# Turning round the product of keys and inputs in a two-branch linear attention kernel, with the gate as a weight column, queries interleaved, and first loads reordered

## The chip, the cores and the metric

The kernel runs on one core of a Trainium2 chip. The metric is the device time of one execution in microseconds (us), as a median of several. A profile of one execution has its own length, called the span; here the time is 1.3 us over the span. Every execution is marked fast or slow (slow: more than 1.5% above the fastest of the same kernel), and fast ones are compared with fast ones.

## The reference

Two linear attention blocks, A and B, read the same x of 2048 x 640. They have their own weights and 32 heads of 20. A gate mixes their outputs.

```python
def block(x, wqkv, wo):                  # A and B alike
    q, k, v = split_heads(x @ wqkv)      # 32 heads of 20
    phi = lambda t: where(t > 0, t + 1, exp(t)) + 1e-6
    pq, pk = phi(q), phi(k)
    kv  = einsum("bhsd,bhse->bhde", pk, v)
    z   = einsum("bhsd->bhd", pk)
    num = einsum("bhqd,bhde->bhqe", pq, kv)
    den = einsum("bhqd,bhd->bhq", pq, z) + 1e-6
    return merge_heads(num / den) @ wo
g = sigmoid((x * gate_w).sum(-1))
return g * block_A(x) + (1 - g) * block_B(x)
```

## The kernel before

The values are never formed. With G = x^T pk, the product of keys and values is pk^T v = G^T Wv, masked to the heads' blocks. This is multiplied by Wo into a matrix WP per block. An output tile is then scaled pq times WP, summed over A and B; the scale holds gate and denominator.

TensorE goes through these stages: 32 key units (5 pairs of a 512- and a 128-column matmul each), 10 G units (16 pairs each) with the small products between them, 40 query units (5 matmuls of 512 columns each), two denominators, 16 output tiles (10 pairs each). ScalarE takes exponentials and copies from PSUM. VectorE finishes phi, sums keys over the sequence, multiplies x by the gate weights, and scales the queries. A small scheduler in Python fixes the order of instructions on each engine when the kernel is built. The queues in the profile are q1 (SP, hardware), q10 (ACT, hardware) and q0 (POOL, software).

The first loads, with cuts:

```python
dma("SP", "x0", XN[:, 0, :], x[0:128, :], ...)
dma("POOL", "cst", CST[:, :], cap[:, :], ...)              # identity and masks
for c in range(NC):
    dma("ACT", "wkA%d" % c, WK["A"][:, c, :], wqkv["A"][...], ...)
dma("SP", "x1", XN[:, 1, :], x[128:256, :], ...)
dma("POOL", "wkB", WK["B"], w3("B", 1), 819200, ...)        # one load of 800 KB
xt_dma(256, 512)                                            # DMA transposes, on SP
xt_dma(512, 1024); xt_dma(1024, 1536); xt_dma(1536, 2048)
dma("SP", "gwb", ...); dma("SP", "xr", XN[:, 2:NT, :], ...) # then WV, WQ, WO
```

G, and the mask of the product of keys and values, with cuts:

```python
def g_unit(X, c):                        # G: rows are inputs, columns keys
    for t in range(NT):
        l = XN[:, t, 128 * c : 128 * c + 128]
        e.matmul(a[:, 0:512], l, PKt[X][:, t, 0:512], ...)
        e.matmul(a[:, 512:D], l, PKt[X][:, t, 512:D], ...)

def kv_unit(X):                          # after the matmuls
    e.tensor_tensor(out=KVL[X][:, us[0] : us[0] + n, :],
        in0=PS[0:GR, ps.slot, 0 : GR * n].rearrange("p (u f) -> p u f", u=n),
        in1=BDM.unsqueeze(1).to_broadcast([GR, n, GR]), op=ALU.mult)
```

The order of TensorE: all G units, then all queries. They must follow, since the finished queries PQ lie in the memory of the keys PK.

Of the kernel before, what the change touches and what calls it, by code (L numbers as in the profile page):

```python
# [7 lines left out]
ALU = mybir.AluOpType  # L8
# [20 lines left out]
def _consts():  # L29
    p = np.arange(128)[:, None]  # L30
    ident = (p == np.arange(128)[None, :]).astype(np.float32)
    bd = (p // 20 == np.arange(GR)[None, :] // 20).astype(np.float32)
    zm = (p // 4 == np.arange(H)[None, :]).astype(np.float32)
    return _bf16_bits(np.concatenate([ident, bd, zm], axis=1))


CW = 128 + GR + H
# [34 lines left out]
class Sched:  # L72
# [12 lines left out]
    def run(self):  # L85
# [26 lines left out]
        while len(self.order) < n:  # L112
# [25 lines left out]
            if o.dma:  # L138
                at[e] = w + o.dma[0]
                o.end = max(w + o.dma[0] + 1500.0, bus[0]) + o.dma[1] / 330.0  # L140
                bus[0] = max(w + o.dma[0] + 1500.0, bus[0]) + o.dma[1] / 330.0
            else:
                o.end = at[e] = w + o.cost
                if e == "PE":
                    o.end += 160.0
# [98 lines left out]
def body(nc, A_x, A_wqkv, A_wo, B_x, B_wqkv, B_wo, gate_w, out, log=None):  # L244
# [9 lines left out]
    XN = sb("XN", [128, NT, D], bf)  # L254
    WKW = sb("WKW", [128, 2 * NU * D], bf)
    WK = {X: WKW[:, i * NC * D : (i + 1) * NC * D].rearrange("p (c f) -> p c f", c=NC) for i, X in enumerate(XS)}
# [5 lines left out]
    PQ = {X: PK[X][:, :].rearrange("p (g s) -> p g s", g=NC) for X in XS}  # L262
# [4 lines left out]
    FX = {(X, b): sb("FX%s%d" % (X, b), [128, 512], bf) for X in XS for b in range(NB)}  # L267
# [4 lines left out]
    ZA = {X: sb("ZA" + X, [128, D], f32) for X in XS}  # L272
    ZH = sb("ZH", [128, 2, D], bf)
# [6 lines left out]
    GWB = sb("GWB", [128, D], bf)  # L280
    GSC = sb("GSC", [128, D], bf)
    LG = sb("LG", [128, NT], f32)
# [12 lines left out]
    BDM = CST[0:GR, 128 : 128 + GR]  # L295
    ZMK = CST[:, 128 + GR : CW]

# [6 lines left out]
    def dma(q, name, dst, src, nbytes, ins=(), outs=(), after=(), issue=450.0, transpose=False):  # L304
        def fn(e):
            d = dst() if callable(dst) else dst
            with nc.allow_non_contiguous_dma(reason="layout"):
                return e.dma_start(d, src() if callable(src) else src, transpose=transpose)

        return op(q, fn, 0.0, ins, outs, after, name=name, dma=(issue, nbytes))  # L310
# [24 lines left out]
    dma("SP", "x0", XN[:, 0, :], x[0:128, :], 163840, outs=[bxn[0]])  # L335
    dma("POOL", "cst", CST[:, :], cap[:, :], 71680, outs=[bcst], issue=700.0)
    for c in range(NC):
        dma("ACT", "wkA%d" % c, WK["A"][:, c, :], wqkv["A"][128 * c : 128 * c + 128, D : 2 * D], 163840, outs=[bwk["A", c]])
    dma("SP", "x1", XN[:, 1, :], x[128:256, :], 163840, outs=[bxn[1]])

    def xt_dma(r0, r1):
        dma(
            "SP",
            "xt%d" % r0,
            XT[:, :, r0:r1],
            x[r0:r1, :],
            (r1 - r0) * D * 2,
            outs=bxt[r0 // 128 : r1 // 128],
            issue=(r1 - r0) * 12.0,
            transpose=True,  # L350
        )
# [4 lines left out]
    dma("POOL", "wkB", WK["B"], w3("B", 1), 819200, outs=[bwk["B", c] for c in range(NC)], issue=900.0)  # L356
    xt_dma(256, 512)
    xt_dma(512, 1024)
    xt_dma(1024, 1536)
    xt_dma(1536, 2048)  # L360
    dma("SP", "gwb", GWB[:, :], gate_w.rearrange("(o n) -> o n", o=1).partition_broadcast(128) if False else gate_w.partition_broadcast(128), 163840, outs=[bgwb])
    dma("SP", "xr", XN[:, 2:NT, :], x[256:S, :].rearrange("(t p) d -> p t d", p=128), 14 * 163840, outs=bxn[2:])
    for X in XS:
        dma("SP", "wv" + X, WV[X][:, :, :], w3(X, 2), 819200, outs=[bwv[X]])
    for X in XS:
        dma("SP", "wq" + X, WQ[X][:, :, :], w3(X, 0), 819200, outs=[bwq[X]])
# [8 lines left out]
    for i in range(7):  # L375
        op(
            "PE",
            lambda e: e.matmul(psw(bw, 512), ONE[:, 0:128], ONE[:, :], start=True, stop=True),
            430.0,
            ins=[bone],  # L380
            outs=[bw],
            name="warm",
        )
    for t in range(2):
        for piece in ((0, 2), (2, 5)):
            bt = Buf("tp", "ps")
            lo, hi = piece
# [16 lines left out]
            def cp(e, t=t, lo=lo, hi=hi, tv=tv):  # L404
                i = tv()[:, 0 : 128 * (hi - lo)].rearrange("p (c s) -> p c s", c=hi - lo)
                o = XT[:, lo:hi, 128 * t : 128 * t + 128]
                if lo == 0:
                    return e.tensor_copy(o, i)
                return e.activation(o, i, ACT.Copy)

            half = Buf("xth")
            op("DVE" if lo == 0 else "ACT", cp, 350.0 if lo == 0 else 510.0, ins=[bt], outs=[half], name="tpc%d" % t)
            bxt[t].halves = getattr(bxt[t], "halves", []) + [half]

# [3 lines left out]
    def k_unit_steps(X, t, ps):  # L418
        def step(c):
            def fn(e):  # L420
                a = psw(ps, D)
                l = XT[:, c, 128 * t : 128 * t + 128]
                e.matmul(a[:, 0:512], l, WK[X][:, c, 0:512], start=(c == 0), stop=(c == NC - 1))  # L423
                return e.matmul(a[:, 512:D], l, WK[X][:, c, 512:D], start=(c == 0), stop=(c == NC - 1))  # L424

            xin = [bxt[t]] if not hasattr(bxt[t], "halves") else [bxt[t].halves[0 if c < 2 else 1]]
            op("PE", fn, mm_cost(512) + mm_cost(128), ins=xin + [bwk[X, c]], outs=[ps], name="k%s%d_%d" % (X, t, c))

        return step

    def k_post(X, t, ps):
# [4 lines left out]
        op("ACT", lambda e: e.activation(EK[:, ek.slot, :], psw(ps, D), ACT.Exp), act_cost(D), ins=[ps], outs=[ek], name="ke")  # L436
# [17 lines left out]
    for X in XS:  # L454
        pss = [Buf("k", "ps", 2) for _ in range(2)]
        st = [k_unit_steps(X, t, pss[t]) for t in range(2)]
        if X == "A":
            for c in range(NC):
                for t in range(2):
                    st[t](c)  # L460
        else:
            for t in range(2):
                for c in range(NC):
                    st[t](c)
        for t in range(2):
            k_post(X, t, pss[t])
    for t in range(2, NT):
        for X in XS:
            ps = Buf("k", "ps", 2)
            s = k_unit_steps(X, t, ps)  # L470
            for c in range(NC):
                s(c)
            k_post(X, t, ps)
# [3 lines left out]
    bsc = None  # L477
    blg = []
    for t in range(NT):
        b = Buf("lg%d" % t)  # L480
        blg.append(b)
        nsc = Buf("gsc")
        op(
            "DVE",
            lambda e, t=t: e.scalar_tensor_tensor(
                GSC[:, :], XN[:, t, :], 1.0, GWB[:, :], op0=ALU.mult, op1=ALU.mult, accum_out=LG[:, t : t + 1]
            ),
            dve1(D) + 100,
            ins=[bxn[t], bgwb] + ([bsc] if bsc else []),
            outs=[b, nsc],  # L490
            prio=LOW + t,
            name="lg",
        )
        bsc = nsc
    bge, bge2, bgg, bgg2, bgt = Buf("ge"), Buf("ge2"), Buf("gg"), Buf("gg2"), Buf("gt")
    op("ACT", lambda e: e.activation(GE[:, :], LG[:, :], ACT.Exp, scale=-1.0), 250.0, ins=blg, outs=[bge], prio=LOW, name="ge")
    op("DVE", lambda e: e.tensor_scalar(GG[:, 1, :], GE[:, :], 1.0, None, op0=ALU.add), 150.0, ins=[bge], outs=[bge2], prio=LOW + 50, name="ge1")
# [5 lines left out]
        ins=[bgg, bge, bge2],  # L503
# [29 lines left out]
    bza = {}  # L533
    for X in XS:
        prev = None
        for t in range(1, NT):
            n = Buf("za%s%d" % (X, t))
            if t == 1:
                f = lambda e, X=X: e.tensor_tensor(out=ZA[X][:, :], in0=PKt[X][:, 0, :], in1=PKt[X][:, 1, :], op=ALU.add)
                ins = [bpk[X, 0], bpk[X, 1]]  # L540
            elif t < NT - 1:
                f = lambda e, X=X, t=t: e.tensor_tensor(out=ZA[X][:, :], in0=ZA[X][:, :], in1=PKt[X][:, t, :], op=ALU.add)
                ins = [prev, bpk[X, t]]
            else:
                f = lambda e, X=X, t=t: e.tensor_tensor(
                    out=ZH[:, XS.index(X), :], in0=ZA[X][:, :], in1=PKt[X][:, t, :], op=ALU.add
                )
                ins = [prev, bpk[X, t]]
            op("DVE", f, dve1(D), ins=ins, outs=[n], prio=LOW + 100 + 20 * XS.index(X) + t, name="za")
            prev = n  # L550
        bza[X] = prev


    bgs = {}

    def g_unit(X, c):
        ps = Buf("g", "ps", 2)
        for t in range(NT):

            def fn(e, t=t):  # L560
                a = psw(ps, D)
                l = XN[:, t, 128 * c : 128 * c + 128]
                e.matmul(a[:, 0:512], l, PKt[X][:, t, 0:512], start=(t == 0), stop=(t == NT - 1))  # L563
# [368 lines left out]
```

## Time and profile before

| | before |
|---|---|
| time, median (3 runs) | 212.49 us |
| span of the profile | 211.6 us |
| first G matmul (end of the key stage) | 64.5 us |
| TensorE waits for key weights | 12.6 us |
| TensorE waits on VectorE, 150 to 168 us | 4.7 us |

The page of the kernel before: the busy line, then rows of 40 equal slices of 5.3 us. A digit is the busy share in tenths; PEclk is the clock granted to TensorE, GB/s what the DMA engines moved.

```profile
PE 190.0 (90%) x1311; PEld 105.9 (50%) x1311; DVE 134.1 (63%) x231; ACT 75.2 (36%) x116; POOL 1.8 (1%) x7
...
PE   5402999999999999999999999999966899999995
...
PEclk9955699999999999999999999999999999999999
DMA  6999999999500002102214045000300015111111
GB/s 182 87 84 123 222 163 318 362 347 239 133 0 3 0 2 60 45 0 61 58 46 151 0 116 179 18 0 26 99 0 0 34 40 176 66 62 62 65 62 64
```

Counted from 1, TensorE is dense but for slices 1 to 4 and a dip at slices 30 to 32. In the first gap the DMA engines are 90% busy, yet move only 84 to 123 GB/s in slices 3 and 4, against some 350 later.

The start in stages (windows). Columns: stretch and length, busy time of TensorE (instructions), granted clock, DMA share (a sum over overlapping packets, so it can pass 1), GB/s.

```profile
core 0: us, PE busy (x), PEclk, DMA share, GB/s
...
9.00:20.00 11.00, 0.14 (x2) 0.59 1.24 108
20.00:24.75 4.75, 4.28 (x15) 0.50 0.98 180
```

From 9 to 20 us TensorE does next to nothing (0.14 us). Then it works at half the clock until 24.75 us.

The same stretch from the SP queue (timeline: start, duration, what was issued):

```profile
0.74 0.89 SPq L308 DMA_DIRECT2D XN<-in_A_x_dram  x2
1.69 26.48 SPq L308 DMA_TRANSPOSE XT<-in_A_x_dram  x4
```

Four transposes take 26.5 us to issue. Looked at singly, the second takes 16.35 us of that, and the last two 3.3 us each.

The queues at 9 to 20 us (packets, MB, time of their packets as a share of the 16 engines):

```profile
q1 hardware_dynamic: 1040, 0.26, 86.3%
q0 software_dynamic: 143, 0.68, 20.9%
q10 hardware_dynamic: 224, 0.25, 16.9%
```

The 1,040 packets of q1, nearly all of the transposes, take 86% of 16 engines for 11 us. That is 0.15 us for a packet of 250 bytes, as a mean. The packed trace, read packet by packet, shows that they are not all slow: half of them took 18 ns, and the 323 that took more than 0.2 us hold 83% of the time.

TensorE's idle places (timeline; in brackets the idle time before the line and what ended it):

```profile
8.43 0.38 PE L423 MATMUL ps<-WKW,XT 128*128 128x512 bf16 x1 [1.23 <-DMA WKW<-in_A_wqkv_dram]
20.03 0.61 PE L423 MATMUL ps<-WKW,XT 128*128 128x512 bf16 x1 [10.89 <-DMA WKW<-in_A_wqkv_dram]
...
156.25 5.59 PE L650 MATMUL ps<-XT,WQB 128*128 128x512 bf16 x25 [2.07 <-DVE PKB L676]
163.74 1.52 PE L820 MATMUL ps<-WPA,PKA 128*128 128x512 bf16 x10 [1.90 <-DVE PKB L676]
167.34 0.39 PE L721 MATMUL ps<-PKA,ZBD 128*32 128x512 bf16 x1 [0.73 <-DVE PKB L676]
```

### The profile page before, as it was taken

How to read it: one execution, taken by the hardware profiler on the slowest of the kernel's cores; microseconds unless marked ns; L12 is line 12 of the kernel's file. 1: busy time of each engine (PE TensorE's matmuls, PEld its weight loads, DVE VectorE, ACT ScalarE, POOL GpSimd, SP SyncE). 2: the span in 40 equal slices, each digit the busy share in tenths (PEclk: the TensorE clock that was granted, in tenths of full speed). 3: DMA queues.
4: the chain of work that ended last, by engine and by line, in shares of the span. 5: the costliest groups of instructions: out<-in, count | busy, mean ns of one | idle time of the engine just before them, and what ended most of it. 6: DMA issues, size and time to landing. Idle time of an engine off the chain costs nothing.

```text
span 211.6 us, 3143 instructions
## 1 busy us (share of the span) xinstructions
PE 190.0 (90%) x1311; PEld 105.9 (50%) x1311; DVE 134.1 (63%) x231; ACT 75.2 (36%) x116; POOL 1.8 (1%) x7
## 2 busy tenths in 40 slices
PE   5402999999999999999999999999966899999995
PEld 1200455555555555575556655545523455555553
DVE  0100488999999999989605878999999674600000
ACT  2100355555552211113333695555236322222222
POOL 3000000000000000000000000000000000000000
PEclk9955699999999999999999999999999999999999
DMA  6999999999500002102214045000300015111111
GB/s 182 87 84 123 222 163 318 362 347 239 133 0 3 0 2 60 45 0 61 58 46 151 0 116 179 18 0 26 99 0 0 34 40 176 66 62 62 65 62 64
DMA packets 22596, 19.86 MB, mean 94 GB/s; under 512 B 10470, under 2 KB 21894, under 8 KB 22582
## 3 DMA queue, kind: packets, MB, share of 16 engines
q1 hardware_dynamic: 21654, 17.95, 35.0%
q10 hardware_dynamic: 720, 0.82, 2.1%
q0 software_dynamic: 208, 0.89, 1.7%
q8 instruction: 10, 0.16, 0.3%
q14 instruction: 4, 0.03, 0.0%
HBM read 12.83 MB, written 4.54 MB: 82 GB/s over the span
## 4 chain that ended last, share of the span: by engine, by line
PE 76%; DVE 12%; DMA 9%; ACTq 1%; issue 0%; ACT 0%; DVEq 0%
PE ps L820 19%; PE ps L563 16%; PE ps L423 16%; PE ps L650 11%; DMA WKW<-in_A_wqkv_dram 9%; PE ps L564 4%; PE ps L424 4%; DVE PKB L676 3%; DVE PKA L676 3%; DVE EQ L668 2%; DVE RCT L751 2%; PE ps L581 2%; DVE PKB L777 1%; DVE PKA L777 1%; PE ps L616 1%; PE ps L721 1%
## 5 line engine op out<-in xcount | busy, mean ns | idle before, releaser
L423 PE MATMUL ps<-WKW,XT 128*128 128x512 bf16 x160 | 45.8, 391 | 12.6 <-DMA WKW<-in_A_wqkv_dram 12.6
L424 PE MATMUL ps<-WKW,XT 128*128 128x128 bf16 x160 | 35.7, 223 | 0.0
L436 ACT ACTIVATE EK<-ps 128x640 bf16<-128x640 f32 x32 | 22.4, 703 | 36.4 <-PE ps L424 36.4
L423 PEld LDWEIGHTS ps<-WKW,XT 128*128 128x128 bf16 x160 | 16.0, 100 | 33.4 <-DMA WKW<-in_A_wqkv_dram 12.2
L665 ACT ACTIVATE EQ<-ps 128x512 bf16<-128x512 f32 x40 | 23.9, 598 | 23.5 <-PE ps L650 13.8
L820 PE MATMUL ps<-WPA,PKA 128*128 128x512 bf16 (+1 forms) x160 | 24.5, 299 | 1.9 <-DVE PKB L676 1.9
L650 PE MATMUL ps<-XT,WQB 128*128 128x512 bf16 x100 | 22.9, 379 | 2.1 <-DVE PKB L676 2.1
L820 PE MATMUL ps<-WPB,PKB 128*128 128x512 bf16 (+1 forms) x160 | 24.5, 299 | 0.0
L439 DVE TENSOR_SCALAR EK<-EK 128x640 bf16<-128x640 bf16 x32 | 10.4, 325 | 20.2 <-ACT EK L436 20.2
L650 PE MATMUL ps<-XT,WQA 128*128 128x512 bf16 x100 | 22.8, 379 | 0.0
L842 ACT ACTIVATE OST<-ps 128x640 bf16<-128x640 f32 (+1 forms) x16 | 11.1, 696 | 32.2 <-PE ps L820 32.2
L563 PE MATMUL ps<-PKB,XN 128*128 128x512 bf16 x80 | 22.3, 379 | 0.0
L563 PE MATMUL ps<-PKA,XN 128*128 128x512 bf16 x80 | 21.8, 379 | 0.0
L668 DVE TENSOR_SCALAR EQ<-EQ 128x512 bf16<-128x512 bf16 x40 | 11.5, 288 | 13.1 <-ACT EQ L665 12.3
L820 PEld LDWEIGHTS ps<-WPA,PKA 128*128 128x128 bf16 x160 | 12.3, 98 | 12.1 <-issue 2.8
L564 PE MATMUL ps<-PKA,XN 128*128 128x128 bf16 x80 | 17.5, 219 | 0.0
L564 PE MATMUL ps<-PKB,XN 128*128 128x128 bf16 x80 | 17.5, 219 | 0.0
L650 PEld LDWEIGHTS ps<-XT,WQB 128*128 128x128 bf16 x100 | 11.4, 118 | 11.7 <-DVE PKB L676 2.5
L820 PEld LDWEIGHTS ps<-WPB,PKB 128*128 128x128 bf16 x160 | 12.3, 98 | 9.4
L840 DVE CAST OST<-ps 128x128 bf16<-128x128 f32 x1 | 0.3, 291 | 26.3 <-PE ps L820 26.3
L650 PEld LDWEIGHTS ps<-XT,WQA 128*128 128x128 bf16 x100 | 11.4, 118 | 9.5 <-issue 0.4
L424 PEld LDWEIGHTS ps<-WKW,XT 128*128 128x128 bf16 x160 | 16.0, 100 | 0.0
(65 smaller groups left out, 199.6 us busy)
## 6 DMA issues: line engine op xcount, KB each, us to landing
out_dram<-OST SPq DMA_DIRECT2D x15, 160.0 KB, 1.8
XN<-in_A_x_dram SPq DMA_DIRECT2D x1, 2240.0 KB, 11.6
WKW<-in_A_wqkv_dram ACTq DMA_DIRECT2D x5, 160.0 KB, 6.6
WKW<-in_B_wqkv_dram POOLq DMA_DIRECT2D x1, 800.0 KB, 19.7
WVA<-in_A_wqkv_dram SPq DMA_DIRECT2D x1, 800.0 KB, 13.4
WVB<-in_B_wqkv_dram SPq DMA_DIRECT2D x1, 800.0 KB, 13.6
WQA<-in_A_wqkv_dram SPq DMA_DIRECT2D x1, 800.0 KB, 11.7
WQB<-in_B_wqkv_dram SPq DMA_DIRECT2D x1, 800.0 KB, 13.0
```

The lines of the kernel that those rows point to most:

```text
L423: e.matmul(a[:, 0:512], l, WK[X][:, c, 0:512], start=(c == 0), stop=(c == NC - 1))
L424: return e.matmul(a[:, 512:D], l, WK[X][:, c, 512:D], start=(c == 0), stop=(c == NC - 1))
L436: op("ACT", lambda e: e.activation(EK[:, ek.slot, :], psw(ps, D), ACT.Exp), act_cost(D), ins=[ps], outs=[ek], name="ke")
L439: lambda e: e.tensor_scalar(EK[:, ek.slot, :], EK[:, ek.slot, :], 1.0, EPS, op0=ALU.min, op1=ALU.add),
L563: e.matmul(a[:, 0:512], l, PKt[X][:, t, 0:512], start=(t == 0), stop=(t == NT - 1))
L564: return e.matmul(a[:, 512:D], l, PKt[X][:, t, 512:D], start=(t == 0), stop=(t == NT - 1))
L650: r = e.matmul(PS[:, ps.slot, :], WQ[X][:, c, g::5], XT[:, c, 512 * b : 512 * b + 512], start=(c == 0), stop=(c == NC - 1),)
L665: op("ACT", lambda e: e.activation(EQ[:, eq.slot, :], PS[:, ps.slot, :], ACT.Exp), act_cost(512), ins=[ps], outs=[eq], name="qe")
L668: lambda e: e.tensor_scalar(EQ[:, eq.slot, :], EQ[:, eq.slot, :], 1.0, EPS, op0=ALU.min, op1=ALU.add),
L676: lambda e: e.scalar_tensor_tensor(PQ[X][:, g, 512 * b : 512 * b + 512], PS[:, ps.slot, :], 0.0, EQ[:, eq.slot, :], op0=ALU.max, op1=ALU.add),
L820: r = e.matmul(a[:, l0 - lo : h0 - lo], PQ[X][:, g, 128 * t : 128 * t + 128], WP[X][:, g, l0:h0], start=(i == 0 and g == 0), stop=(i == 1 ...
L842: op("ACT", lambda e, w=w, ps=ps, os_=os_: e.activation(OST[:, os_.slot, 0:w], psw(ps, w), ACT.Copy), act_cost(w), ins=[ps], outs=[os_], n ...
```

## The change

Its intent: shorten the start; take the sums of keys and the gate products (39 us) off VectorE; move queries forward among the G units, so that VectorE isn't flooded later.

- The key weights go in single chunks over the SP and ACT queues, ahead of all transposes. A third tile of x is transposed by TensorE.
- G^T is computed. Strided slices of pk are stationary and x moves, with a column of ones that gives z. The result is copied out and turned back by ten DMA transposes from SBUF to SBUF.
- gate_w is a 641st column of B's key weights; the gate's exponential reads it from PSUM.
- Queries have memory of their own at first, so 25 of 40 units go among the G units. The scalings are put at fixed places in VectorE's order.
- The rows of the product are now ordered by g and m (key 5m+g). The mask multiplication puts them back.

The main edits, with cuts:

```diff
+    dma("ACT", "cst", CST[:, :], cap[:, :], 128 * CW * 2, outs=[bcst])
+    ld_x("SP", 1)
+    ld_wk("ACT", "A", 0)
+    ld_wk("SP", "A", 1)
+    ld_wk("ACT", "A", 2)
+    ld_x("SP", 2)
+    ld_wk("ACT", "A", 4)
+    ld_wk("SP", "A", 3)
+    dma("ACT", "gw", GW5[:, :], ...)
+    for c in range(NC):
+        ld_wk("SP", "B", c)
+    for t0, t1 in ((3, 4), (4, 5), (5, 6), (6, 8), (8, 12), (12, 16)):
+        xt_dma(t0, t1)
 ... (in g_unit)
-                l = XN[:, t, 128 * c : 128 * c + 128]
-                e.matmul(a[:, 0:512], l, PKt[X][:, t, 0:512], ...)
+                l = PKt[X][:, t, g::5]
+                e.matmul(a[:, 0:512], l, XN[:, t, 0:512], ...)
+                return e.matmul(a[:, 512 : D + 1], l, XN[:, t, 512 : D + 1], ...)
+        dma("SP", ..., GS[X][:, :, 128 * g : 128 * g + 128], GTS[X][:, g, :], transpose=True)
 ... (in kv_unit)
-                    out=KVL[X][:, us[0] : us[0] + n, :],
+                    out=KVL[X][:, us[0] : us[0] + n, :].rearrange("p u (m g) -> p u g m", g=NC),
 ... (order; the sums of keys, the gate products and z_unit are gone)
+    for g in range(NC):
+        g_unit("A", g); q_next(3)
+    for g in range(NC):
+        g_unit("B", g); q_next(2)
+        ...                                  # A's products at g = 1 to 4
+    q_next(1); den(0); q_next(3)
+    kv_unit("B"); q_next(3)
+    for u in range(NU):
+        wp_unit("B", u)
+        if u % 2: q_next(1)
+    wp_back("B"); q_next(1); scale_now(0); q_next(4)
+    out_unit(0); scale_now(1); den(1)
```

## The prediction

> **What bounds it now.** TensorE: busy 190.0 of 211.6 us (busy table). The span cut into stages (windows) shows three losses.
> 1. Start. The key projection issues only 6 of its 160 matmul pairs by 9 us, waits for the A key weights until 20.0 us (waits: 12.6 us, longest 10.9), and runs at a granted clock of 0.50 until 24.75. The culprit is not volume: the DMA view moves 353 GB/s at 3 to 5 us, but 108 GB/s at 9 to 20 us with the engines busy. The second DMA transpose, issued beside weight loads still in flight on two other queues, holds its queue for 16.35 us; the last two take 3.3 us each. The Trainium skill ("DMA: Bandwidth & Descriptors", Issuing engines are not separate DMA queues) says that all queues share the same 16 engines; this agrees.
> 2. 150 to 168.5 us: VectorE is over 95% busy (reciprocal 3.35 us, scaling 1.49 us each, query post-processing 0.98 us per unit against 1.08 us of TensorE); TensorE loses 4.7 us.
> 3. The tail after the last matmul, 2.0 us.
>
> Elsewhere TensorE is dense: a 512+128 pair is 0.271 us, 160 pairs 43.4 us; a query unit is 1.08 us.
>
> **What the change does.**
> - First loads: weights go ahead of all transposes on two hardware queues. 2.2 MB at 353 GB/s from 2.2 us: A weights by about 7 us, B by 9 us; then the transposes run alone, 13 tiles at about 1 us each (a 4-tile one now issues in 3.3 us and lands in 5.9). The first transposed tile is needed near 13.5 us, then one per 2.7 us, so they keep ahead. The key stage should start at 5.2 us, lose 1 to 2 us in arrivals, and end near 50 us, against 64.5 now: minus 14.5 us, all on the critical path and nearly all of the gain.
> - G^T has the same 160 pairs (129 columns for 128). Stationary slices now step by 5. The Trainium skill ("TensorE: Matmul & The Clock Gate", Weight-path perf modes) allows fast weight load at such steps. In the trace, ten strided loads feeding one-column matmuls pass in 0.36 us, so I expect the pair to stay at 0.27 us.
> - The sums of keys (30 x 0.82 us) and the gate products (16 x 0.9 us) leave VectorE: 39 us, none on the path. ScalarE gains 16 small exponentials (about 0.2 us each). Worth nearly nothing; dropping the z matmuls saves 0.36 us.
> - Ten SBUF transposes of 164 KB, about 4 us each to landing, with 8 us or more of other TensorE work ahead of their use: hidden.
> - 25 query units move among G, out of the VectorE-bound stage. But after the first denominator VectorE still owes 14 units, the reciprocal, masks and two scalings: 22.6 us, against 18.4 us of TensorE. Before the first output tile they are about equal. I expect 3 us (0 to 6) of stall to remain of the 4.7.
>
> **Sum.** Key stage ends 50; then 139.9 us of dense work (145.1 now, less 4.9 stall, 0.36 z); 3 stall; 2 tail: span 195. The time is about 1 us over the span: 196 us. Range 191.5 to 201.5. Chances: faster 0.96, same 0.03, slower 0.01.
>
> **Right if** the wait for key weights falls below 2 us, the first G matmul starts at 49 to 52 us, its pair stays at 0.27 us, VectorE busy falls to about 97 us, and stalls around the first output tile total 0 to 6 us.
>
> **Wrong if** transposes again starve other loads, or single-tile ones are slower than 2.7 us; strided weights slow the pair; the SBUF transposes arrive late or block the queue; or VectorE's fixed order stalls the denominators.

## The result

| | before | after |
|---|---|---|
| time, median of 4 runs | 211.92 us | 198.9 us (198.56 to 199.23) |
| span | 211.6 us | 197.5 us |
| first G matmul | 64.5 us | 50.4 us |
| first G matmul to the last copy out of PSUM | 145.1 us | 144.3 us |
| last copy's start to the end | 2.0 us | 2.8 us |

The ratio is 0.942 (95% interval 0.934 to 0.949). Ratios here divide the mean time of one kernel's fast runs by that of the other's of the same rounds, so they are not quite the ratio of the medians.

The gain is 14.1 us before the first G matmul. All the rest of the change gives 0.8 us, and the tail takes that back.

The same lines of the changed kernel. First its page:

```profile
PE 186.8 (95%) x1280; PEld 108.6 (55%) x1305; DVE 103.3 (52%) x183; ACT 77.0 (39%) x129; POOL 0.4 (0%) x6
...
PE   6799999999999999999999999995998999999994
...
PEclk9999999999999999999999999999999999999999
DMA  5999999990033110110110312341650043110212
GB/s 177 291 175 206 301 381 363 239 204 13 5 67 75 38 33 0 33 33 3 33 33 3 95 33 62 78 166 53 201 178 36 33 144 126 66 66 35 68 66 68
```

The gap at the start has gone and the clock is full throughout. VectorE has lost 31 us of work. The dip of TensorE remains, now at slices 28 and 31.

Its start in stages (columns as above):

```profile
9.00:20.00 11.00, 10.89 (x81) 1.00 1.00 182
20.00:24.75 4.75, 4.70 (x36) 1.00 0.99 303
```

The stretch from 9 to 20 us now holds 10.9 us of TensorE work.

Its SP queue:

```profile
0.73 0.87 SPq L325 DMA_DIRECT2D XN<-in_A_x_dram  x2
...
3.12 2.34 SPq L325 DMA_DIRECT2D WKW<-in_B_wqkv_dram  x5
5.50 13.26 SPq L325 DMA_TRANSPOSE XT<-in_A_x_dram  x6
```

Thirteen tiles are transposed in 13.3 us, about 1.0 us each.

Its queues at 9 to 20 us:

```profile
q1 hardware_dynamic: 7861, 1.99, 99.4%
```

q1 again keeps the engines busy, but with 7,861 packets of 250 bytes: 0.022 us for each on average, against 0.15 before.

Its idle places on TensorE after the warm-up:

```profile
6.88 0.39 PE L470 MATMUL ps<-WKW,XT 128*128 128x512 bf16 x1 [1.32 <-DMA WKW<-in_A_wqkv_dram]
...
137.41 0.40 PE L678 MATMUL ps<-WOB,KVLB 120*120 120x512 bf16 x1 [1.87 <-DVE PKA L738]
138.25 0.43 PE L678 MATMUL ps<-WOB,KVLB 120*120 120x512 bf16 x1 [0.38 <-DVE PKA L738]
149.65 1.52 PE L861 MATMUL ps<-WPA,EX 128*128 128x512 bf16 x10 [0.94 <-DMA WPB<-wpdB]
153.88 1.31 PE L861 MATMUL ps<-WPA,EX 128*128 128x128 bf16 x9 [0.16 <-issue]
```

The 4.7 us of waits before have become 3.4 us in four places. Two more idle stretches of 0.4 us before G units show only in the weight loads' row. Against the best version at the end, where TensorE hardly waits and the same stretch takes 139.7 us, the loss is 4.6 us here. Before it was about 5.4 us.

The strided stationary slices, in the groups view (count, busy us, mean ns of one, idle before). Before:

```profile
L563 PEld LDWEIGHTS ps<-PKA,XN 128*128 128x128 bf16 x80 | 7.8, 98 | 9.5
L564 PE MATMUL ps<-PKA,XN 128*128 128x128 bf16 x80 | 17.5, 219 | 0.0
```

After:

```profile
L603 PEld LDWEIGHTS ps<-XN,PKA 128*128 128x128 bf16 x80 | 9.4, 117 | 7.9
L604 PE MATMUL ps<-XN,PKA 128*128 128x129 bf16 x80 | 17.6, 220 | 0.3
```

A weight load takes 117 ns for 98, but a pair still starts every 0.272 us, against 0.271.

### The profile page after: what moved, and what is told of

Read it like the earlier page. It is cut to its first block, busy times and chain, and to the rows that moved or that the text cites. A ratio compares the mean times of both kernels' runs of the same rounds, so it can differ in the third digit from the quotient of the medians.

```text
span 197.5 us, 3082 instructions
## 1 busy us (share of the span) xinstructions
PE 186.8 (95%) x1280; PEld 108.6 (55%) x1305; DVE 103.3 (52%) x183; ACT 77.0 (39%) x129; POOL 0.4 (0%) x6
## 4 chain that ended last, share of the span: by engine, by line
PE 84%; DMA 6%; DVE 4%; ACT 2%; issue 1%; SPq 0%; DVEq 0%
PE ps L861 22%; PE ps L470 17%; PE ps L603 17%; PE ps L712 15%; PE ps L604 5%; PE ps L471 5%; DMA WKW<-in_A_wqkv_dram 3%; DMA WPB<-wpdB 2%; DVE PKA L738 2%; PE ps L642 1%; ACT WKW L690 1%; PE ps L762 1%; ACT EQ L727 1%; DVE KVLB L657 1%; DMA wpdB<-WKW 1%
## 5 line engine op out<-in xcount | busy, mean ns | idle before, releaser
L470 PE MATMUL ps<-WKW,XT 128*128 128x512 bf16 x154 | 43.0, 379 | 1.3 <-DMA WKW<-in_A_wqkv_dram 1.3
L471 PE MATMUL ps<-WKW,XT 128*128 128x128 bf16 (+1 forms) x160 | 35.1, 220 | 0.3
L603 PE MATMUL ps<-XN,PKB 128*128 128x512 bf16 x76 | 21.7, 380 | 0.2
L610 ACT ACTIVATE WKW<-ps 128x640 bf16<-128x640 f32 x10 | 7.0, 703 | 38.0 <-PE ps L604 38.0
L603 PE MATMUL ps<-XN,PKA 128*128 128x512 bf16 x75 | 21.5, 379 | 0.0
L604 PE MATMUL ps<-XN,PKA 128*128 128x129 bf16 x80 | 17.6, 220 | 0.3
L604 PE MATMUL ps<-XN,PKB 128*128 128x129 bf16 x80 | 17.6, 220 | 0.2
L738 DVE SCALAR_TENSOR_TENSOR PKA<-ps,EQ 128x512 bf16<-128x512 f32 x20 | 13.8, 691 | 0.7
L603 PEld LDWEIGHTS ps<-XN,PKB 128*128 128x128 bf16 x80 | 9.4, 117 | 8.4 <-DVE PKA L738 0.8
L603 PEld LDWEIGHTS ps<-XN,PKA 128*128 128x128 bf16 x80 | 9.4, 117 | 7.9
## 6 DMA issues: line engine op xcount, KB each, us to landing
WQA<-in_A_wqkv_dram SPq DMA_DIRECT2D x1, 800.0 KB, 10.9
```

The costliest lines, as they stand in the source:

```text
L470: e.matmul(a[:, 0:512], l, WK[X][:, c, 0:512], start=(c == 0), stop=(c == NC - 1))
L471: return e.matmul(a[:, 512:w], l, WK[X][:, c, 512:w], start=(c == 0), stop=(c == NC - 1))
L603: e.matmul(a[:, 0:512], l, XN[:, t, 0:512], start=(t == 0), stop=(t == NT - 1))
L604: return e.matmul(a[:, 512 : D + 1], l, XN[:, t, 512 : D + 1], start=(t == 0), stop=(t == NT - 1))
L610: op("ACT", lambda e: e.activation(GTS[X][:, g, :], psw(ps, D), ACT.Copy), act_cost(D), ins=[ps], outs=[b], name="gc")
L738: lambda e: e.scalar_tensor_tensor(PQ[X, b][:, g, :], PS[:, ps.slot, :], 0.0, EQ[:, eq.slot, :], op0=ALU.max, op1=ALU.add),
```

## The experiments

Each call also ran the kernel before on the same chip: medians of 213.3 us (e1 to e4), 212.2 (r1 to r4) and 211.7 (t1 to t4). In the last call its runs spread from 206.67 to 213.93 us, and only two of eleven count as fast. That call's kernels are therefore compared with one another.

### e1: only the new load order, in the kernel before

```diff
 (kernel before: first loads replaced by the new ones; two tiles of x by TensorE as before)
+    for t0, t1 in ((2, 3), (3, 4), (4, 5), (5, 6), (6, 8), (8, 12), (12, 16)):
+        xt_dma(t0, t1)
```

> The kernel before, with nothing changed but the order and queues of the first loads (constants first, A and B key weights in single chunks on the two hardware queues, transposes after them). Theory 1 (the load order alone is the gain): the wait for A key weights falls from 12.6 us to under 2 us, the first G matmul starts at 50 to 52 us instead of 64.5, and the time is 198 to 200 us, within 1% of the changed kernel. Rival (VectorE, which still has the 39 us of sums and gate products, holds the earlier key stage or the stage of the queries back): 203 us or more, with TensorE waits on VectorE of 5 us or more above the 4.7 of before.

Measured: 198.46 us (198.07 to 198.63), first G matmul at 50.1 us, wait for key weights 1.2 us. From there to the last copy 145.1 us, as in the kernel before. Theory 1 held. The loads alone give the whole gain, with all 39 us of sums and gate products still on VectorE.

### e2: the changed kernel with the old load order, nearly

```diff
 (changed kernel)
+    (old order and queues; x tile 2 loaded on SP before the transposes)
+    for t0, t1 in ((3, 4), (4, 8), (8, 12), (12, 16)):
```

> The changed kernel with the old order of first loads (constants and B key weights on the software queue, transposes straight after three tiles of x). Theory 1: the wait for key weights comes back, 9 to 13 us, and the time is 210 to 213 us, within 1% of the kernel before: all other parts of the change together are worth under 2 us. Rival (the other parts are worth something by themselves): 207 us or less although the wait is back.

Measured: 201.55 us, first G matmul at 52.2 us. The long wait did not come back. Both expectations missed what happened: the order differs from the old one by one plain load and a first transpose of one tile, and that let the weights through. (The rival's 207 us or less came out, but without the wait that it assumed.) Two of the three queues at 7 to 9 us:

```profile
q1 hardware_dynamic: 536, 0.13, 62.7%
q0 software_dynamic: 83, 0.34, 46.3%
```

Transposes and the software queue's load are in flight together here too, and a transpose packet takes 0.037 us on average, not 0.15. So their meeting alone, at this point, does not bring the long wait. r4 below takes this up.

### e3: B's key weights on the other hardware queue

```diff
-    dma("POOL", "wkB", WK["B"], ...)
+    dma("ACT", "wkB", WK["B"], ...)
```

> The kernel before, B key weights issued on the scalar hardware queue after the A weights instead of on the software queue; transposes still first on the sync queue. Theory 1a (transposes side by side with any ordinary load on another queue go slowly and starve it): the wait for A weights stays at 8 us or more and the time stays above 207 us. Rival 1b (the software queue is the culprit): the wait falls under 4 us and the time to 199 to 203 us.

Measured: 203.86 us, first G matmul at 55.2 us. The waits left at the start:

```profile
10.28 0.39 PE L423 MATMUL ps<-WKW,XT 128*128 128x512 bf16 x1 [2.55 <-DMA WKW<-in_A_wqkv_dram]
13.14 0.61 PE L423 MATMUL ps<-WKW,XT 128*128 128x512 bf16 x1 [1.59 <-DMA WKW<-in_B_wqkv_dram]
```

With the transposes still first and still overlapping the weights, 9 us of the loss went away by moving one load off the software queue. The idle time is 4.1 us (2.55 for A weights and 1.59 for B), not 12.6. So rival 1b was nearer than 1a, though its upper limit of 203 us was just missed. The queues at 9 to 12 us, when B's load runs beside the transposes:

```profile
q10 hardware_dynamic: 630, 0.78, 85.4%
q1 hardware_dynamic: 280, 0.06, 37.2%
```

A transpose packet takes 0.064 us on average here. The edit changes two things at once: the kind of the queue, and that B's load now follows the A weights on one queue and no longer runs beside them. No run parts these two.

### e4: transposes held until the weights have landed

```diff
-            outs=bxt[r0 // 128 : r1 // 128],
+            outs=bxt[r0 // 128 : r1 // 128], after=held,   # held: wkA0..4 and wkB
```

> The kernel before, everything on its old queues, but the sync queue waits for all key weights before it issues the first transpose. Theory 1a (overlap of transposes and loads is what costs): key weights all landed by 9 to 11 us, no wait for A weights over 2 us, transposes then take 3.3 to 4 us per four tiles, and the time falls to 198 to 203 us though the transposes start 7 us later. Rival (transposes are slow at this point whatever runs beside them, or the constants on the software queue set the start): the key stage now waits for transposed x instead, and the time stays above 207 us.

Measured: 200.33 us. The software queue kept its load, and the transposes started at 10.3 us:

```profile
10.27 13.15 SPq L308 DMA_TRANSPOSE XT<-in_A_x_dram  x4
```

They then took 13.2 us for 14 tiles, and no wait for A weights exceeded 1.44 us. So the software queue does no harm by itself either. In these kernels the loss needs both: transposes in flight together with the load of the software queue. With that load behind the A weights on a hardware queue (e3) they cost much less. Both together are not enough, as e2 shows. Why some of the transposes' packets take so long in the kernel before isn't shown by these runs.

### r1: the changed kernel again, as reference

> The changed kernel once more, as the reference for the three runs beside it. Every theory: 198.5 to 199.3 us.

Measured: 199.6 us (198.51 to 201.88, the highest one slow), a little above what was expected. The five fast runs have two levels: 198.5 to 199.2 us at a granted clock of 1.0, and 200.1 to 200.6 at 0.991. r3 shows where the second level arises.

### r2: the mask product with a contiguous write

The permutation moves to the side that reads PSUM; the mask's broadcast moves with it.

```diff
-    out=KVL[X][...].rearrange("p u (m g) -> p u g m", g=NC),
-    in0=PS[...].rearrange("p (u g m) -> p u g m", u=n, g=NC),
-    in1=BDM.unsqueeze(1).unsqueeze(1).to_broadcast([GR, n, NC, 24]),
+    out=KVL[X][...].rearrange("p u (m g) -> p u m g", g=NC),
+    in0=PS[...].rearrange("p (u g m) -> p u m g", u=n, g=NC),
+    in1=BDM.unsqueeze(1).unsqueeze(3).to_broadcast([GR, n, 24, NC]),
```

> The changed kernel, with the multiplication by the block mask written so that its output is contiguous and the permutation is on the side that reads PSUM (it took 1.50 and 0.92 us per matrix with the permuted write, 0.65 and 0.40 us in the kernel before). Theory 2 (the permuted write doubles it, and in the B case this sits in VectorE's queue ahead of the stall before the second product of weights): 0.65 and 0.40 us again, the TensorE stall of 1.87 us at 137 us falls by about 1.4 us, and the time falls by 0.5 to 1.4 us. Rival (the four-dimensional pattern with its short runs costs this on either side): 1.3 us or more for the larger one, time within 0.3 us.

The two instructions for B on VectorE's timeline, in the kernel before, the changed kernel and r2:

```profile
115.15 0.96 DVE L596 TENSOR_TENSOR KVLB<-ps,CST 120x480 bf16<-120x480 f32 x2
```

```profile
131.80 2.18 DVE L657 TENSOR_TENSOR KVLB<-ps,CST 120x480 bf16<-120x480 f32 x2 [0.38 <-PE ps L642]
```

```profile
131.84 0.97 DVE L657 TENSOR_TENSOR KVLB<-ps,CST 120x480 bf16<-120x480 f32 x2 [0.38 <-PE ps L642]
```

The mask product had grown from 0.96 to 2.18 us, and is 0.97 us again. The stall at 137 us fell from 1.87 to 0.75 us. From the first G matmul to the last copy took 143.0 us, 1.3 less than in the changed kernel. In the timed runs the gain is not resolved: 199.2 us against r1's 199.6, with the start's spread on top. The mechanism of theory 2 is seen in the profile; its effect on the time is within the noise here.

### r3: 46 idle multiplications added to VectorE

```diff
+    for i, (X, t) in enumerate([...]):      # 46 of them, lowest priority
+        op("DVE", lambda e, ...: e.scalar_tensor_tensor(GSC[:, :], PKt[X][:, t, :], 1.0,
+           PKt[X][:, t, :], op0=ALU.mult, op1=ALU.mult, accum_out=LG[:, i : i + 1]), ...)
```

> The changed kernel with 46 extra VectorE multiplications of 128 by 640 (0.9 us each, results unused, at the lowest priority), as much VectorE work as the change took away. Theory 3 (the removed 39 us were off the path): VectorE busy rises from 103 to about 143 us and the time changes by less than 0.6 us. Rival (taking them away is what lets the queries be interleaved without stalls): 1.5 us or more slower, with TensorE waits on VectorE between 88 and 150 us.

Measured: 199.59 us against 199.6; at a granted clock of 1.0 two runs of 197.84 and 197.88. VectorE busy 138.9 us. Theory 3 held: the work taken off VectorE was not on the path.

The profile of this run fell in a fast execution of the second level. TensorE in stages (columns as above):

```profile
130.00:138.00 8.00, 6.17 (x51) 1.00 0.29 112
138.00:142.00 4.00, 3.53 (x10) 0.63 0.65 204
```

The 1.87 us stall just before 138.09 us and the 0.38 us one after it are there in every profile of the changed kernel. In this execution the clock then falls, to a mean of 0.63 for 4 us: in the trace's clock record it is 0.5 for 3.41 us from 139.0 us. The profiles of t1 (a slow execution) and of r4 have the same two stalls, and a stretch of 3.41 us at 0.5 that begins within 1.2 us of the first one's end. The other profiles with this order of work (the changed kernel, r1, e2) have the stalls and no such stretch. So such a stall sometimes costs about its length a second time. What decides it isn't shown.

### r4: the changed kernel with exactly the old load order

```diff
+    (as e2, but x tile 2 not loaded apart and not transposed by TensorE)
+    for t0, t1 in ((2, 4), (4, 8), (8, 12), (12, 16)):
```

> The changed kernel with exactly the old order of first loads: two tiles of x by TensorE, the first transpose (two tiles) third on the sync queue at 1.7 us, not fourth at 2.1 us and of one tile as in the run that came out at 201.6 us. Theory 4 (the long wait needs the transpose's packets to meet the software queue's weight load at its beginning; the 0.45 us and one more plain load ahead of the transposes let the weights through): the wait for key weights is back at 9 us or more, first G matmul at 60 us or later, time 209 to 213 us. Rival (something else in the changed kernel, such as fewer or shorter loads, lets the weights through): 204 us or less.

Measured: 214.29 us, ratio to before 1.012 (1.006 to 1.018), first G matmul at 65.7 us. TensorE's long wait and the SP queue:

```profile
20.71 0.18 PE L446 MATMUL ps<-CST,GW 5*128 5x5 bf16 x1 [11.22 <-DMA GW<-in_gate_w_dram]
```

```profile
1.66 25.66 SPq L325 DMA_TRANSPOSE XT<-in_A_x_dram  x4
```

The wait is back in full. It is named after the gate weights, which follow the A weights on the ACT queue and stand before them in TensorE's order. Theory 4 held in the wait and in the first G matmul; the time is 1.3 us above its upper limit. With the old loads, everything else in the change is worth nothing, or slightly less. e2 and r4 differ by one plain load (of x tile 2) ahead of the transposes, with it by 0.45 us in their start, and by the size of the first one; and by 13 us in the time. Which of these lets the weights through was not separated.

### t1 and t2: changed kernel beside the loads-only kernel

> The changed kernel a third time, as the reference beside the next three. 198.5 to 199.7 us.

> The kernel before with only the new order of first loads, again, now beside the changed kernel on the same chip. Theory 1 (the loads are the whole gain; G^T, the gate column and the interleaving together are worth nothing as they stand): within 0.6 us of the changed kernel, either side. Rival: the changed kernel is faster by 1.5 us or more.

Measured: 200.07 us for the changed kernel (fast runs 197.7 to 200.36) and 198.11 us for the loads-only kernel (197.32 to 198.55). The best runs differ by 0.4 us, the medians by 2: outside the 0.6 us of theory 1, but in favour of the loads-only kernel. Four of the six runs of the changed kernel were of its second level. Four of the loads-only kernel's runs show a clock of 0.991 too, and its fastest is one of them. In its profile the half clock (3.41 us from 142.8 us) again follows a stall for VectorE, of 2.08 us. But the next wait for VectorE is then 0.21 us, where e1, with no half clock, has 1.90: the lost time was absorbed there. The rival's 1.5 us in favour of the changed kernel did not show.

### t3: all queries after G again

On top of r2. A's products stay among the G units of B.

```diff
     for g in range(NC):
-        g_unit("A", g); q_next(3)
+        g_unit("A", g)
     ...                                      # likewise for B
+    q_next(4); kv_unit("B"); q_next(2)
+    ...                                      # B's six units, a query after every second
+    wp_back("B"); q_next(13); den(0); q_next(14); scale_now(0); q_next(4)
+    out_unit(0); scale_now(1); den(1)
```

> The changed kernel with the contiguous write of the mask product (which measured 1 us less in its span), and with all queries after G again, as in the kernel before. Theory 5 (interleaving does cut the stalls of TensorE, from about 5 to 3 us, once the mask product is cheap): stalls of about 4.5 to 5.5 us between 120 and 155 us, time 0.5 to 2.5 us above the 199.2 of the same kernel with interleaved queries, so 199.5 to 201. Rival (interleaving is worth nothing, because the units it leaves after the first denominator still wait for VectorE): within 0.4 us of 199.2.

Measured: 196.34 us (196.0 to 196.94), first G matmul to last copy 142.1 us. Its waits:

```profile
146.42 1.52 PE L861 MATMUL ps<-WPA,EX 128*128 128x512 bf16 x10 [1.30 <-DVE EX L818]
...
150.03 0.40 PE L762 MATMUL ps<-PKA,ZBD 128*32 128x512 bf16 x3 [0.74 <-DVE PKB L738]
```

Both expectations missed, and in the other direction: without interleaving the kernel is not slower, but in these runs faster than r2 (197.57 to 199.63). It was run at another time. B's product is back long before it is needed, with 31 query units behind it. As the change interleaved them, queries that had covered the chain of B's product had been moved ahead of that chain. That t3 also loses less than the kernel before (2.4 us against 5.4 in this stretch), although it too has its queries after G, I put down to the scalings: two of them stand before the first output tile, where the kernel before has four in a row (5.6 us). This was argued from the two timelines, not tested alone. t3 also has the first denominator after 22 query units and behind B's product, not after 26 and ahead of it; the two moves were not parted.

### t4: a better order

On top of r2: A's products one G unit earlier and ahead of the queries there; 18 query units after the first denominator, nine of them behind B's product as cover; the second denominator after two output tiles. The scheduler's cost estimate for the reciprocal also goes from 3900 to 3400 ns, which can shift VectorE's order; it is not in the cut below.

```diff
-        g_unit("A", g); q_next(3)
+        g_unit("A", g); q_next((0, 0, 2, 4, 5)[g])
     ...
-        g_unit("B", g); q_next(2); ...       # A's product at g = 1
+        g_unit("B", g); ...; q_next((0, 2, 3, 1, 2)[g])   # A's product at g = 0
-    q_next(1); den(0); q_next(3); kv_unit("B"); q_next(3)
+    q_next(3); den(0); q_next(1); kv_unit("B"); q_next(3)
     ...                                      # B's six units, 2, 1, 0, 1, 1, 0 queries after them
-    wp_back("B"); q_next(1); scale_now(0); q_next(4)
-    out_unit(0); scale_now(1); den(1)
+    wp_back("B"); scale_now(0); q_next(9)
+    out_unit(0); scale_now(1); out_unit(1); den(1)
```

> A version meant to beat both: contiguous write of the mask product, the A product of keys and values directly after the first G unit of B, its weight products between the later G units and ahead of the queries there, only 18 query units left after the first denominator but with the second denominator after two output tiles, not one. Same matrix work. If the 4.8 us of stalls in the changed kernel between 100 and 155 us come from the order of work around VectorE's reciprocal and from the readback of the B product, as the waits say: stalls there under 1.5 us, span 193 to 194.5 us, time 194.5 to 196 us. Rival (VectorE has too much work from the first denominator on, whatever the order): stalls of 3 us or more, time above 197.5 us.

Measured: 193.97 us; five of six runs lie between 193.9 and 194.03. After 110 us the matmul row shows a single wait:

```profile
122.17 1.03 PE L712 MATMUL ps<-XT,WQA 128*128 128x512 bf16 x4 [0.18 <-issue]
```

The time is under the 194.5 to 196 us that were expected. From the first G matmul to the last copy it takes 139.7 us, 4.6 less than in the changed kernel; 1.3 of these are r2's write, the other 3.3 come with the order. These stalls came from the order of work, not from too much of it on VectorE. This version beats both: the changed kernel beside it had 197.7 us at best, the kernel before 206.67.

## Why the prediction was right or wrong

The time, 198.9 us, lies in the range of 191.5 to 201.5 and 2.9 us above the point. Point by point:

- **The start, the whole gain: right.** It said that the key stage would end near 50 us; it ended at 50.4. The wait for A weights was to fall below 2 us; it was 1.3. Tiles were to be transposed at 1 us each; they were. e1 shows that this alone makes the time, and r4 that without it nothing is left.
- **Its reason: too wide.** It blamed the overlap of a transpose with loads on two other queues. e3 and e4 show that the overlap with the load on the software queue is what was so dear (9 us of the loss; e3 leaves open whether by the kind of queue or by that load's place beside the A weights), and that neither does it alone; e2 shows that even both together need not. That all queues share 16 engines, which the Trainium skill says ("DMA: Bandwidth & Descriptors", Issuing engines are not separate DMA queues), is not enough to explain this. The predicted time did not hang on this reason, because the change removed the overlap and the software queue at once.
- **Strided slices: right.** The pair stayed at 0.272 us, as fast weight load at such steps in the Trainium skill ("TensorE: Matmul & The Clock Gate", Weight-path perf modes) lets one expect. Whether that mode was on isn't shown; the loads took 117 ns for 98.
- **39 us off VectorE is worth nothing: right** (e1, r3). Its busy time was put at 97 us and was 103. The mask products (2.7 us more), ten small products for z (2.4 us) and more copies of x (1.3 us) had been left out.
- **SBUF transposes hidden: right.** They land in 2.6 us, less than the 4 estimated, and no TensorE wait is named after them.
- **"I expect 3 us (0 to 6) of stall to remain of the 4.7": mis-sized.** It was 4.6 us. Three terms were missed. The masks were carried over at their old cost but took 2.18 us for B; r2 shows that this is the permuted write, and gets back 1.1 us of stall. The readback of B's product cost 0.94 us, with the cover of queries gone. Two G units waited 0.4 us each. Interleaving was credited with the remaining gain; t3 shows that as built it gives none. (The prediction's "over 95% busy" for VectorE holds from 150 to 166 us, with 15.58 of 16 us; up to 168.5 us it is 91%.)
- **Tail and offset: 1.1 us short.** 2.8 us of tail for 2. The last write of 32 KB landed in 2.3 to 2.4 us here and in t3 and t4, and in 1.6 in the kernel before, e1, r3 and r4; the cause is open. The time is 1.3 us over the span, not 1.

The sum of the misses in the span: 0.4 (start) + 1.6 (stalls) + 0.8 (tail) - 0.2 (dense work: 139.7 for 139.9) = 2.6 us of the 2.5 between 195 and 197.5.

## What to carry to other kernels

Before transposing by DMA at the start, let the weights go first: in the profile, a queue whose issue takes many times its usual length while the engines are busy and move little is the sign, and holding it back (e4) or changing the load order alone (e1) tells what it costs. Taking work off an engine or moving it forward pays only where a wait for it ends last; work moved forward may have been the cover for another chain, so ask what stood behind it. A permutation that is free in one operand may double the cost in another, so read the new duration of every instruction that got a new access pattern.

## What the Trainium skill lacked or had wrong

- "DMA: Bandwidth & Descriptors", Rules for kernel authors, says that "A transpose next to ordinary DMAs needs nothing". That held for correct results in every run here, but not for time: in the kernel before, with a software-queue load in flight, transpose packets took 0.15 us on average instead of 0.022, and the kernel 9 us longer than with the same load on a hardware queue behind the A weights (213.3 against 203.9 us). In e2 such a load was in flight too, and they took 0.037 us.
- The same page, Issuing engines are not separate DMA queues, says that issuing on several engines saves only sequencer time. Here moving one load to another queue, behind the loads there, was worth those 9 us.
- The same page, Latency and other measured facts, gives 261 GB/s for DMA transposes with a non-contiguous middle dimension on one kernel, and more for the contiguous case. In the changed kernel, 13 tiles of 164 KB on one queue took 13.3 us to issue, which is 160 GB/s.
- "SBUF — State Buffer", Door 1: The DMA port swizzle, explains that each SBUF access that crosses to a new 16-byte line costs extra, and that non-contiguous PSUM access slows matmuls. On VectorE a bf16 write at a 10-byte step cost 2.18 us for 0.96, while reading fp32 from PSUM at a 96-byte step cost nothing (0.97 us; r2 changed the mask's pattern with it). No page gives these VectorE figures.
- "TensorE: Matmul & The Clock Gate", Why this matters for your kernels, warns of idle gaps over about 3 us. Here a gap of 1.87 us followed soon by one of 0.38 us was followed, in some executions, by a mean clock of 0.63 over 4 us (r3; the same two gaps and 3.41 us of half clock in r4).
- The same page, Weight-path perf modes, allows steps between weights, but gives no cost: loads at a step of 5 took 117 ns for 98, hidden behind the matmuls.
